# Delta rule and two expert layers on one core: the first chunks' chain in a given order, ten weights loaded at once, and the min of the first block on ScalarE

## The chip, the cores and the metric

One core of one Trainium2 chip runs the kernel. The metric is the device time of one execution in microseconds. The engines are TensorE (PE, with its weight loads as PEld), VectorE (DVE), ScalarE (ACT), GpSimd (POOL) and SyncE (SP), which issues every DMA.

## What is computed

A delta rule over 768 tokens for 4 batches of 8 heads (head size 48), then two expert layers on the 3072 tokens of width 384 that it gives, each through a hidden width of 2048. All in float32.

```python
for t in range(S):
    y[:, :, t] = einsum('bhd,bhde->bhe', q[:, :, t], state)
    v_old = einsum('bhde,bhd->bhe', state, k_n[:, :, t])
    state = state + beta * einsum('bhd,bhe->bhde', k_n[:, :, t], v[:, :, t] - v_old)
# layer 1: g = h where h >= 1, 0 where h <= -1, else (h + 1)**2 / 4
# layer 2: g = max(h, 0)**2;  both: h = x @ w_in, then g @ w_out
```

## The kernel before

The sequence is cut into 24 chunks of 32 tokens; a chunk holds 4 batches x 32 tokens on 128 partitions. Inside a chunk the recurrence is a triangular system. Chunks are taken in groups (`GROUPS`, the first of 2 chunks, the second of 4), and one triangle of 32 x 32 per partition is solved for a whole group by `tri` (L334): a transpose in (`begin`, L351), norms, two scalings (`row`, `row2`), 30 steps of a multiply and an add (`step`, L411 and L412), a transpose out (`end`, L415). Triangle 0 (group 0) is solved by VectorE in two halves of 16 with one instruction for both (`two`), 14 steps of 28 instructions, and the halves are joined by small matmuls (`joined`, L424: `ld` and `dld`, L437 to L450). The other triangles run on GpSimd.

`gram` (L268) makes the k and q products of a chunk on TensorE, and a mask cuts them (L297). For the grams of group 1 and the q halves of chunks 0 and 1, ScalarE first copies the product out (L294) and GpSimd masks the copy. `chunk_steps` (L457) is the chain of a chunk: `ks`, `tr`, `qs`, `pu`, `ku`, `xt`; each is 64 small matmuls and a copy or subtraction by ScalarE or VectorE. Chunks 0 and 1 form block 0 and are done before the first layer starts; chunk 1 takes its dependence on chunk 0 from `cross_gram`.

Layer 1 runs over blocks of 2 or 3 chunks (`SIZES`), for each over 16 slices f of the hidden width: `hidden` (L565) makes one slice with 9 matmuls (a float32 number is held as two parts, so three products) and the activation, and `out1` two slices later multiplies it into the output. Before the change the activation is: ScalarE `r = relu(h + 1)` (L581), VectorE `g = min(r, 2) / 2` (L582), ScalarE `g * g` (L583), VectorE `max(r - 1, g)` (L584), then a ScalarE cast and a VectorE subtraction (L592, L593) for the two parts. The blocks share a ring of three tiles for r and g.

The weights lie in HBM as 64-bit floats. Each of the 32 tiles of layer 1 (16 slices, i = 0 for w_in and 1 for w_out) is loaded by `load_w` and converted in four stages that `flow` staggers by one step each: ScalarE Prelu (L164), two VectorE operations (L172, L175), ScalarE cast (L186), VectorE subtraction (L190). `more_w1` runs one such step. `first1(EAGER)` issues the first 18 loads; each conversion then allows a load up to 8 ahead (`AHEAD`). Layer 1's loads go to the slot of the weight itself; layer 2's to a ring of three raw buffers. The slots of late weights (`spare`) hold the small tiles of the first chunks until then.

The order of the work: up to the norms of triangle 1 every engine issues in the order in which the program is written (`manual_schedule`). After that only TensorE does, and the order on the other engines and on SP is made by a planner from its own model of time. In that part the chain of chunks 0 and 1 runs with 4 x 3 conversion steps between its pieces, then the blocks. Work beside the blocks hangs on slots, two to a slice, 32 to a block: one conversion step a slot in block 0, grams of group 2 at slots 4, 7, 10 and 13, the chains of block 1 from slot 19 (`HEAD`). `later` puts work behind the marked operations `marks[0]` (ScalarE's relu) and `marks[1]` (VectorE's min) on their engines; `tc.issue_after(x)` orders behind x on x's engine and waits for nothing.

Of the kernel before, what the change touches and what calls it, by code (L numbers as in the profile page):

```python
# [25 lines left out]
def kernel(  # L26
# [38 lines left out]
    EAGER = 18  # L65
    AHEAD = 8
# [48 lines left out]
    kqt, kvt, gp, nt, xh, xl = {}, {}, {}, {}, {}, {}  # L115

# [31 lines left out]
    raws = {}  # L148


    def load_w(x, key):
# [30 lines left out]
    def part_stages(key, box):  # L182
# [13 lines left out]
    def weight_items(w):  # L196
# [5 lines left out]
        def item(x):  # L202
            _, f, i = keys[x]
            box = {}
            if w == 0:
                r = part_stages(keys[x], box)
# [4 lines left out]
            r[1] = lambda: (s1(), ahead(x + 1 + (RAW if w else AHEAD)))  # L211
# [5 lines left out]
        def ahead(end):  # L217
            while todo and todo[0][0] < end:
                load_w(*todo.pop(0))
# [48 lines left out]
    def gram(c, lo=0, hi=2, late=0, eng=None):  # L268
# [18 lines left out]
        if c >= KQ:  # L287
            kqg.pop(c)
            if late < 2:
                load_kg(c + KG)  # L290
# [22 lines left out]
    spare = {  # L313
        name: f"w{i}{NF - f}" for name, i, f in
        (("u0", 1, 1), ("u1", 1, 2), ("cross", 0, 1), ("z", 1, 3), ("l", 0, 2), ("d", 1, 4))
    }
# [17 lines left out]
    def tri(n, eng, halves=False):  # L334
# [9 lines left out]
        def two(t, rows, cols):  # L344

            a = t[:, rows, cols]
            (ps_, p_), (rs_, r_), (cs_, c_) = a.ap
            return bass.AP(a.tensor, a.offset, [[ps_, p_], [T2 * (T + 1), 2], [rs_, r_], [cs_, c_]])

# [5 lines left out]
        both = slice(0, T2)  # L355
# [16 lines left out]

        def row():
            if halves:
                d = two(gm, both, both)
                eng.tensor_mul(
                    d, d, r.rearrange("p (a o i) -> p a o i", a=2, o=1)
                    .to_broadcast([P, 2, T2, T2]))
                return
            for e, rs, cs in whole:  # L380
                e.tensor_mul(gm[:, rs, cs], gm[:, rs, cs], across(r, rs, cs))

        def row2():
            if halves:
                eng.tensor_mul(
                    two(x, both, both), two(gm, both, both),
                    g.rearrange("p (a i o) -> p a i o", a=2, o=1).to_broadcast([P, 2, T2, T2]))
            else:
                for e, rs, cs in whole:
                    e.tensor_mul(x[:, rs, cs], gm[:, rs, cs], down(g, rs, cs))  # L390
# [5 lines left out]
        def step(j):  # L396
            if halves:
                w = T2 - 1 - j
                t = ring.tile([P, 2, j, w], F32, tag="t0", bufs=1, name="t")
                rest = two(x, slice(0, j), slice(j + 1, T2))  # L400
                by = two(x, slice(0, j), slice(j, j + 1))
                of = two(gm, slice(j, j + 1), slice(j + 1, T2))
                shape = [P, 2, j, w]
            else:
                w = T - 1 - j
                t = ring.tile([P, j, w], F32, tag="t0", bufs=1, name="t")
                rest = x[:, 0:j, j + 1:T]
                by = x[:, 0:j, j:j + 1]
                of = gm[:, j:j + 1, j + 1:T]
                shape = [P, j, w]  # L410
            eng.tensor_mul(t, by.to_broadcast(shape), of.to_broadcast(shape))  # L411
            eng.tensor_add(rest, rest, t)  # L412
# [150 lines left out]
    marks = [None, None, None]  # L563

    def hidden(layer, n, f):  # L565
# [12 lines left out]
        if layer == 0:  # L578
# [85 lines left out]

    V, G = nc.vector, nc.gpsimd
# [14 lines left out]
    with tc.manual_schedule():  # L680
# [27 lines left out]
        begin, pre, steps, end = tri(0, V, True)  # L708
# [10 lines left out]
        go(masks)  # L719
        end()  # L720
        rows0()
        begin, pre, steps, end1 = tri(1, G)
        begin()
        ins = go(pre[:-2])
        behind[0] = lambda: tc.issue_after(ins.ins)
    ENGINES = {mybir.EngineType.PE}
    with tc.manual_schedule(engines=ENGINES):
        for f in (ld0, dld0):
            for c in range(HEADS):
                f(c)  # L730
        go(pre[-2:])
        go(steps)
        chains = [chunk_steps(c) for c in range(HEADS)]
        (k0, t0, q0, p0, _, x0), (k1, t1_, q1, p1, _, x1) = chains
        for m, fs in enumerate([[k0, t0], [k1], [q0, p0], [t1_], [q1], [x0], [p1], [x1]]):
            go(fs)
            if m < 4:
                more_w1(3)
# [51 lines left out]
        for c in range(HEADS):  # L790
            put(0, 8 + 4 * c, lambda c=c: load_kq(c + KQ))
# [115 lines left out]
```

## Time and profile before

| | |
|---|---|
| median of 3 runs | 1054.86 us (1054.44 to 1056.35) |
| the profiled execution | 1054.6 us |
| its span, first to last instruction | 1052.9 us |
| mean granted TensorE clock | 0.99 of full speed |
| busy in the span | PE 989.3, DVE 611.5, ACT 454.3, POOL 313.2 us |
| all weight loads | 64 of 384 KB, median 6.3 us to land |

A row of the trace has the start in us, the length, the engine, the line, the operation, output<-input and the count; brackets hold the idle time of the engine before it and what ended it, where "issue" means that nothing in the profile was waited for. A row of a group has, after the bar, busy us, mean ns of one, and the idle time before.

### The profile page before, as it was taken

Reading aid. Unit: us, or ns where it says so; the run is one execution under the profiler, and the core shown is the slowest. Engines: PE = TensorE matmul, PEld = TensorE weight load, DVE = VectorE, ACT = ScalarE, POOL = GpSimd, SP = SyncE. Lnnn points to the kernel's source line nnn. Section 1 sums busy time; section 2 is a strip of 40 time slices with the busy share of each in tenths; the row PEclk is TensorE's granted clock in tenths of the full one; section 3 lists DMA queues with packets and bytes.
Section 4 is the critical chain, followed back from the end, with each engine's and each line's share of the span. In section 5 each row is a group of like instructions: output and inputs, shape, how many; then the busy total and the mean of one; then the engine's idle time right before and its main releaser. Section 6 shows DMA issues by size and latency. Waiting matters only on the chain.

```text
span 1052.9 us, 33012 instructions
## 1 busy us (share of the span) xinstructions
PE 989.3 (94%) x14440; PEld 945.0 (90%) x14440; DVE 611.5 (58%) x1125; ACT 454.3 (43%) x931; POOL 313.2 (30%) x456
## 2 busy tenths in 40 slices
PE   4358898999999999999999999999999999999998
PEld 4347788898899998999999999999999999999998
DVE  6879765675575666767545577543434343444333
ACT  2346544445444444545445554433333333333332
POOL 4690681294039208608600123110101010010000
PEclk9997999999999999999999999999999999999999
DMA  9942144352451441512111223010101010000000
GB/s 297 326 121 77 33 124 134 88 150 73 130 152 48 148 134 33 167 56 70 31 42 55 77 90 121 16 45 1 45 1 46 1 45 1 24 1 24 1 23 23
DMA packets 36049, 80.89 MB, mean 77 GB/s; under 512 B 4544, under 2 KB 18368, under 8 KB 35904
## 3 DMA queue, kind: packets, MB, share of 16 engines
q1 hardware_dynamic: 35904, 78.78, 24.8%
q8 instruction: 113, 1.85, 0.8%
q14 instruction: 32, 0.26, 0.1%
HBM read 63.03 MB, written 15.73 MB: 75 GB/s over the span
## 4 chain that ended last, share of the span: by engine, by line
PE 81%; DVE 11%; issue 4%; ACT 2%; DMA 1%; SPq 0%; DVEq 0%; ACTq 0%
PE acc L555 36%; PE h L555 35%; PE tr L486 2%; PE yy L506 2%; PE sps L517 2%; PE yy L472 2%; DVE g L582 1%; DVE g L584 1%; PE g L281 1%; PE ks L472 1%; DVE gl L593 1%; DVE wl L172 1%; DVE wl L175 1%; DVE gp L415 1%; PE xt L540 1%
## 5 line engine op out<-in xcount | busy, mean ns | idle before, releaser
L555 PE MATMUL h<-xh,w 128*128 128x384 f32 (+1 forms) x1632 | 320.4, 332 | 1.8 <-ACT r L581 1.3
L555 PEld LDWEIGHTS h<-xh,w 128*128 128x128 f32 x1632 | 272.7, 190 | 6.8 <-ACT r L581 1.8
L593 DVE TENSOR_TENSOR gl<-g,gh 128x384 fp32r<-128x384 f32 (+1 forms) x272 | 169.5, 623 | 134.3 <-ACT gh L592 128.8
L592 ACT CAST gh<-g 128x384 fp32r<-128x384 f32 (+1 forms) x272 | 135.0, 496 | 209.3 <-DVE g L584 106.0
L555 PE MATMUL h<-xl,w 128*128 128x384 f32 (+1 forms) x816 | 179.8, 329 | 1.3 <-DVE xl L543 1.3
L555 PE MATMUL acc<-gh,w 128*128 128x384 f32 (+1 forms) x864 | 168.5, 331 | 3.8 <-ACT gh L592 3.8
L587 DVE TENSOR_TENSOR g<-r 128x384 f32<-128x384 f32 x128 | 71.4, 558 | 157.4 <-ACT r L586 157.4
L555 PE MATMUL acc<-w,gh 128*128 128x384 f32 x768 | 155.6, 337 | 2.0 <-DVE e L600 2.0
L586 ACT ACTIVATE r<-h,zero 128x384 f32<-128x384 f32 x128 | 74.5, 582 | 166.1 <-PE h L555 166.1
L555 PEld LDWEIGHTS acc<-gh,w 128*128 128x128 f32 x864 | 136.9, 191 | 9.8 <-ACT gh L592 4.2
L555 PEld LDWEIGHTS h<-xl,w 128*128 128x128 f32 x816 | 141.5, 190 | 1.9 <-DVE xl L543 1.9
L555 PEld LDWEIGHTS acc<-w,gh 128*128 128x128 f32 x768 | 136.3, 188 | 2.3 <-ACT gh L592 2.3
L581 ACT ACTIVATE r<-h,one 128x384 f32<-128x384 f32 (+1 forms) x144 | 78.6, 546 | 89.4 <-PE h L555 84.9
L411 POOL TENSOR_TENSOR t<-tx,gm 128x30 f32<-128x30 f32 (+9 forms) x180 | 109.6, 609 | 19.9 <-DVE tx L390 6.4
L412 POOL TENSOR_TENSOR tx<-tx,t 128x30 f32<-128x30 f32 (+9 forms) x180 | 108.4, 602 | 13.7
L584 DVE SCALAR_TENSOR_TENSOR g<-r,g 128x384 f32<-128x384 f32 (+1 forms) x144 | 88.8, 617 | 36.6 <-ACT g L583 34.8
L582 DVE TENSOR_SCALAR g<-r 128x384 f32<-128x384 f32 (+1 forms) x144 | 63.6, 442 | 79.5 <-ACT r L581 78.9
L642 POOL CAST xh<-x2r 128x1152 fp32r<-128x1152 f32 x8 | 9.5, 1186 | 292.9 <-PE h L555 246.1
L583 ACT ACTIVATE g<-g 128x384 f32<-128x384 f32 (+1 forms) x144 | 70.6, 490 | 59.4 <-DVE g L582 58.3
L555 PE MATMUL acc<-gl,w 128*128 128x384 f32 (+1 forms) x432 | 91.5, 320 | 2.6 <-DVE gl L593 2.6
L555 PE MATMUL acc<-w,gl 128*128 128x384 f32 x384 | 88.0, 337 | 0.0
L555 PEld LDWEIGHTS acc<-gl,w 128*128 128x128 f32 x432 | 72.4, 190 | 3.3 <-DVE gl L593 3.3
(94 smaller groups left out, 835.9 us busy)
## 6 DMA issues: line engine op xcount, KB each, us to landing
raw<-in_w_dram SPq DMA_DIRECT2D x64, 384.0 KB, 6.3
kqt<-in_kq_dram SPq DMA_DIRECT2D x88, 192.0 KB, 3.8
kv<-in_kv_dram SPq DMA_DIRECT2D x24, 384.0 KB, 3.1
w2f<-wl SPq DMA_DIRECT2D x32, 192.0 KB, 3.5
w2r<-w2f SPq DMA_DIRECT2D x16, 384.0 KB, 3.0
x2r<-x SPq DMA_DIRECT2D x8, 576.0 KB, 4.4
out_dram<-e SPq DMA_DIRECT2D x24, 192.0 KB, 2.0
x<-e SPq DMA_DIRECT2D x18, 192.0 KB, 2.3
```

The source lines that it names most:

```text
L411: eng.tensor_mul(t, by.to_broadcast(shape), of.to_broadcast(shape))
L412: eng.tensor_add(rest, rest, t)
L472: per_bh(lambda b, h, p, pd: nc.tensor.matmul(o[p, h], kqt[c][pd, b // 2, h, x * T:(x + 1) * T], st[pd, b // 2, h], start=h == 0, stop=x = ...
L555: nc.tensor.matmul(o, *((r, l) if swap else (l, r)), **flags)
L581: marks[0] = nc.scalar.activation(r, h, AF.Relu, bias=one)
L582: marks[1] = nc.vector.tensor_scalar(g, r, 2.0, 0.5, ALU.min, ALU.mult)
L583: nc.scalar.activation(g, g, AF.Square)
L584: nc.vector.scalar_tensor_tensor(g, r, -1.0, g, ALU.add, ALU.max)
L586: marks[0] = nc.scalar.activation(r, h, AF.Relu, bias=zero)
L587: marks[1] = nc.vector.tensor_mul(g, r, r)
L592: nc.scalar.copy(ghi, g)
L593: nc.vector.tensor_sub(glo, g, ghi.bitcast(F32))
```

## The change

In the prelude every engine now keeps the written order through the whole chain of chunks 0 and 1. Ten weights are loaded at first; no other until the eleventh, whose slot (`w14`) is the one that the cross tile uses, and the loads of k, q and v that come later are issued behind that one on SP. From the eighteenth weight (`OWN`) loads go to the ring of three raw buffers. Six conversion steps in place of twelve stand among the chain, and the conversions may run three loads ahead. From the twentieth (`ALONE`) on, the last subtraction of a conversion is GpSimd's. The masks of the prelude are VectorE's. Triangle 0 is solved half by VectorE and half by GpSimd. In block 0 the min becomes `relu(1 - r / 2)` on ScalarE, and the square is taken of one minus that; the mark for `later` is then the VectorE max.

```diff
-    EAGER = 18
-    AHEAD = 8
+    EAGER = 10
+    OWN = 17
+    ALONE = 20
...
-        if w == 0:
+        if w == 0 and x < OWN:
             pool, tag, bufs = wp, f"w{i}{f}", 1
         raw = raws[key] = pool.tile([P, DM, 2], I32, tag=tag, bufs=bufs, name="raw")
-        nc.sync.dma_start(raw.rearrange("p a b -> p (a b)"), (w1, w2)[w][f, i].bitcast(I32))
+        with after[0]():
+            ins = nc.sync.dma_start(
+                raw.rearrange("p a b -> p (a b)"), (w1, w2)[w][f, i].bitcast(I32)
+            )
+        if w == 0 and x == EAGER:
+            after[0] = lambda: tc.issue_after(ins.ins)
...
-            nc.vector.tensor_sub(lo, box["t"], hi.bitcast(F32))
+            (nc.vector if x < ALONE else nc.gpsimd).tensor_sub(lo, box["t"], hi.bitcast(F32))
...
-            r[1] = lambda: (s1(), ahead(x + 1 + (RAW if w else AHEAD)))
+            r[1] = lambda: (s1(), ahead(x + 1 + RAW))
...
         def ahead(end):
+            if w == 0 and turn[0] is not None:
+                end = min(end, EAGER)
...
+    spare = {"cross": f"w1{EAGER // 2 - 1}"}
+    for x, name in enumerate(("u0", "u1", "z", "l", "d", "t")):
+        spare[name] = f"w{x % 2}{NF - 1 - x // 2}"
...
+        parts = whole
+        if halves:
+            parts = [(e, *[slice(T2 * i, T2 * i + T2)] * 2) for i, e in enumerate(halves)]
...
+            for i, e in enumerate(halves or (eng,)):
+                lo, hi = (T2 * i, T2 * i + T2) if halves else (0, T)
+                w = hi - lo - 1 - j
...
+            for e, lo, hi, t in ts:
+                rest = x[:, lo:lo + j, lo + j + 1:hi]
+                e.tensor_add(rest, rest, t)
...
-            marks[1] = nc.vector.tensor_scalar(g, r, 2.0, 0.5, ALU.min, ALU.mult)
-            nc.scalar.activation(g, g, AF.Square)
-            nc.vector.scalar_tensor_tensor(g, r, -1.0, g, ALU.add, ALU.max)
+            if n:
+                marks[1] = nc.vector.tensor_scalar(g, r, 2.0, 0.5, ALU.min, ALU.mult)
+                nc.scalar.activation(g, g, AF.Square)
+            else:
+
+                nc.scalar.activation(g, r, AF.Relu, scale=-0.5, bias=one)
+                nc.scalar.activation(g, g, AF.Square, scale=-1.0, bias=one)
+            last = nc.vector.scalar_tensor_tensor(g, r, -1.0, g, ALU.add, ALU.max)
+            if not n:
+                marks[1] = last
...
-        begin, pre, steps, end = tri(0, V, True)
+        begin, pre, steps, end = tri(0, V, (V, G))
...
-        go([gram(c, late=2, eng=G) for c in range(GFIRST[1], GFIRST[2])])
+        masks1 = [gram(c, late=2) for c in range(GFIRST[1], GFIRST[2])]
         cross_gram(0, 1)
-        masks = [gram(c, 1, 2, late=2, eng=G) for c in range(HEADS)]
+        masks = [gram(c, 1, 2, late=2) for c in range(HEADS)]
         go(steps)
         for c in range(HEADS):
             value(c)
-        go(masks)
+
+        rows0()
         end()
-        rows0()
+        for c in range(HEADS):
+            ld0(c)
+        go(masks1)
+        for c in range(HEADS):
+            dld0(c)
+        chains = [chunk_steps(c) for c in range(HEADS)]
+        (k0, t0, q0, p0, _, x0), (k1, t1_, q1, p1, _, x1) = chains
+        go([k0, t0])
         begin, pre, steps, end1 = tri(1, G)
         begin()
-        ins = go(pre[:-2])
-        behind[0] = lambda: tc.issue_after(ins.ins)
+        go(masks)
+        k1()
+        go(pre[:-2])
+        go([q0, p0, t1_])
+        go(pre[-2:])
+        go(steps)
+        more_w1(2)
+        q1()
+        x0()
+        more_w1(2)
+        p1()
+        more_w1(1)
+        x1()
+        more_w1(1)
...
         turn[0] = None
-        load_kv(HEADS)
+        first1(EAGER + RAW)
+        quiet(load_kv, HEADS)
         for c in range(KG):
-            load_kg(KQ + KG + c)
+            quiet(load_kg, KQ + KG + c)
...
-            put(0, 8 + 4 * c, lambda c=c: load_kq(c + KQ))
+            put(0, 8 + 4 * c, lambda c=c: quiet(load_kq, c + KQ))
```

## Rows read from the trace of the kernel before

**Rows 1.** Stretches: length; busy (count) PE, PEld, DVE, ACT, POOL; clock; DMA share; GB/s.

```profile
27.00:65.70 38.70, 16.24 (x744) 14.13 (x744) 30.23 (x50) 14.60 (x33) 28.74 (x44) 1.00 0.88 266
65.70:81.00 15.30, 9.16 (x161) 8.45 (x161) 15.30 (x25) 6.94 (x16) 13.68 (x23) 0.86 0.26 80
81.00:101.40 20.40, 17.11 (x267) 15.36 (x267) 20.25 (x52) 15.57 (x38) 0.83 (x1) 0.77 0.28 80
101.40:120.00 18.60, 15.39 (x339) 14.33 (x337) 17.54 (x41) 9.40 (x24) 7.53 (x6) 0.91 0.10 24
120.00:138.00 18.00, 17.66 (x538) 16.10 (x538) 8.87 (x20) 8.80 (x21) 15.88 (x28) 1.00 0.26 69
...
58.00:60.00 2.00, 0.91 (x47) 0.72 (x36) 1.67 (x2) 1.21 (x3) 1.84 (x3) 1.00 0.27 106
```

**Rows 2.** TensorE in order of time, 30 to 66 us: start, length, idle before and reason.

```profile
33.07 1.52 PE L437 MATMUL z<-d,l 32*32 32x16 f32 x98 [2.31 <-issue]
41.19 1.52 PE L445 MATMUL w<-gp,z 32*32 32x16 f32 x98 [6.21 <-issue]
48.36 1.00 PE L486 MATMUL tr<-kv,gp 32*32 32x48 f32 x34 [5.03 <-issue]
56.13 0.92 PE L506 MATMUL yy<-u,gp 32*32 32x48 f32 x34 [4.07 <-issue]
60.34 1.00 PE L466 MATMUL yy<-u,cross 32*32 32x48 f32 x35 [1.43 <-issue]
65.68 0.58 PE L555 MATMUL h<-xh,w 128*128 128x256 f32 x1 [0.57 <-ACT xh L542]
```

**Rows 3.** DMA of the first 60 us: the instruction queue; the weight loads (us to landing).

```profile
q8 instruction: 8, 0.13, 1.0%
raw<-in_w_dram SPq DMA_DIRECT2D x32, 384.0 KB, 8.2
```

**Rows 4.** VectorE and GpSimd in order of time, 15 to 27 us.

```profile
15.19 0.18 DVE L411 TENSOR_TENSOR t<-tx,gm 128x28 f32<-128x28 f32 x1
19.64 2.52 POOL L297 TENSOR_TENSOR gp<-gp,mask 128x512 f32<-128x512 f32 x2 [6.41 <-ACT gp L294]
19.67 1.36 DVE L411 TENSOR_TENSOR t<-tx,gm 128x108 f32<-128x108 f32 x1
26.71 0.21 DVE L412 TENSOR_TENSOR tx<-tx,t 128x28 f32<-128x28 f32 x1
```

**Rows 5.** GpSimd by line (busy, mean ns, idle before): 119 to 124, 37.3 to 41.2 us.

```profile
L411 POOL TENSOR_TENSOR t<-tx,gm 128x58 f32<-128x58 f32 x1 | 0.3, 290 | 0.1
L411 POOL TENSOR_TENSOR t<-tx,gm 128x58 f32<-128x58 f32 x1 | 0.5, 480 | 0.1
```

**Rows 6.** VectorE by line: 27 to 65.7 us; after the dots 80 to 101 us.

```profile
L175 DVE SCALAR_TENSOR_TENSOR wl<-wt,wl 128x384 int32<-128x384 int32 x11 | 8.6, 800 | 0.0
L190 DVE TENSOR_TENSOR w<-wl,w 128x384 fp32r<-128x384 f32 x9 | 7.7, 852 | 0.0
L172 DVE TENSOR_SCALAR wl<-raw 128x384 int32<-128x384 uint32 x11 | 6.6, 617 | 0.0
...
L175 DVE SCALAR_TENSOR_TENSOR wl<-wt,wl 128x384 int32<-128x384 int32 x13 | 7.3, 565 | 0.0
L190 DVE TENSOR_TENSOR w<-wl,w 128x384 fp32r<-128x384 f32 x12 | 6.8, 569 | 0.0
L172 DVE TENSOR_SCALAR wl<-raw 128x384 int32<-128x384 uint32 x11 | 3.9, 354 | 0.0
L584 DVE SCALAR_TENSOR_TENSOR g<-r,g 128x256 f32<-128x256 f32 x5 | 2.1, 421 | 0.0
L582 DVE TENSOR_SCALAR g<-r 128x256 f32<-128x256 f32 x5 | 1.5, 296 | 0.0
```

**Rows 7.** ScalarE by line, 65.7 to 101.4 us.

```profile
L581 ACT ACTIVATE r<-h,one 128x256 f32<-128x256 f32 x7 | 3.3, 466 | 2.8 <-PE h L555 2.4 <-DVE gl L593 0.4
```

**Rows 8.** The raw weight tile, 130 to 400 us: its loads.

```profile
DMA to landing us min/median/max: 3.0/3.5/5.3
```

More of the change, by code (lines that the diff above doesn't have):

```diff
@@ L115 @@
     kqt, kvt, gp, nt, xh, xl = {}, {}, {}, {}, {}, {}
+    marks = [None] * 3
     def load_kq(c):
@@ L148 @@
     raws = {}
+    after = [nullcontext]
     def load_w(x, key):
@@ L179, in convert_stages, with part_stages @@
         return [s0, s1]
-    def part_stages(key, box):
+    def part_stages(x, key, box):
         _, f, i = key
@@ L205, in item @@
             if w == 0:
-                r = part_stages(keys[x], box)
+                r = part_stages(x, keys[x], box)
             else:
@@ L288, in gram @@
             kqg.pop(c)
-            if late < 2:
+            if turn[0] is None:
                 load_kg(c + KG)
@@ L311 @@
     cross = {}
[L313 to L316, printed above, removed]
+    spare = {"cross": f"w1{EAGER // 2 - 1}"}
+    for x, name in enumerate(("u0", "u1", "z", "l", "d", "t")):
+        spare[name] = f"w{x % 2}{NF - 1 - x // 2}"
     def cross_gram(a, c):
@@ L332, with tri @@
     T2 = T // 2
-    def tri(n, eng, halves=False):
+    def tri(n, eng, halves=()):
         x = tx
@@ L342, in flat @@
             return t.rearrange("p j i -> p (j i)")[:, diag]
[L344 to L348, printed above, removed]
         def begin():
@@ L371, in gamma2 @@
             return nc.vector.tensor_mul(g, g, bet[:, n, :])
+        parts = whole
+        if halves:
+            parts = [(e, *[slice(T2 * i, T2 * i + T2)] * 2) for i, e in enumerate(halves)]
         def row():
[L374 to L380, printed above, removed]
+            for e, rs, cs in parts:
                 e.tensor_mul(gm[:, rs, cs], gm[:, rs, cs], across(r, rs, cs))
         def row2():
[L384 to L390, printed above, removed]
+            for e, rs, cs in parts:
+                e.tensor_mul(x[:, rs, cs], gm[:, rs, cs], down(g, rs, cs))
             nc.vector.tensor_copy(flat(x), g)
@@ L396, in step @@
         def step(j):
[L397 to L412, printed above, removed]
+            ts = []
+            for i, e in enumerate(halves or (eng,)):
+                lo, hi = (T2 * i, T2 * i + T2) if halves else (0, T)
+                w = hi - lo - 1 - j
+                pool, tag = (wp, spare["t"]) if i else (ring, "t0")
+                t = pool.tile([P, j, w], F32, tag=tag, bufs=1, name="t")
+                ts.append((e, lo, hi, t))
+                e.tensor_mul(
+                    t,
+                    x[:, lo:lo + j, lo + j:lo + j + 1].to_broadcast([P, j, w]),
+                    gm[:, lo + j:lo + j + 1, lo + j + 1:hi].to_broadcast([P, j, w]),
+                )
+            for e, lo, hi, t in ts:
+                rest = x[:, lo:lo + j, lo + j + 1:hi]
+                e.tensor_add(rest, rest, t)
         def end():
@@ L663, in go, with quiet @@
         return r
+    def quiet(load, c):
+        with after[0]():
+            load(c)
     V, G = nc.vector, nc.gpsimd
@@ L718 @@
             value(c)
-        go(masks)
+        rows0()
         end()
-        rows0()
+        for c in range(HEADS):
[6 more added lines that the diff above has]
+        go([k0, t0])
         begin, pre, steps, end1 = tri(1, G)
         begin()
-        ins = go(pre[:-2])
-        behind[0] = lambda: tc.issue_after(ins.ins)
+        go(masks)
[12 more added lines that the diff above has]
+        more_w1(1)
     ENGINES = {mybir.EngineType.PE}
     with tc.manual_schedule(engines=ENGINES):
[L728 to L738, printed above, removed]
         behind[0] = lambda ins=marks[2]: tc.issue_after(ins.ins)
         turn[0] = None
-        load_kv(HEADS)
+        first1(EAGER + RAW)
+        quiet(load_kv, HEADS)
         for c in range(KG):
-            load_kg(KQ + KG + c)
+            quiet(load_kg, KQ + KG + c)
         SL = 2 * NF
```

2 lines of the change are left out of this document (removed).

## The prediction

> **What bounds the kernel now.** I read the table of busy time by stretch first [rows 1]. From 120 us on TensorE is busy 17.66 of 18.00 us, so there is nothing to win behind that point except what is carried into it: whatever is saved before it shifts the rest. Up to 65.7 us, where the first block's first matmul starts [rows 2], it is another kernel: TensorE is busy 16.24 of 38.70 us, the DMA engines have a share of 0.88, and VectorE, busy 30.23, is the fullest engine. From 65.7 to 101.4 VectorE has no gap worth the name (15.30 of 15.30, 20.25 of 20.40), and TensorE's granted clock falls to 0.86 and 0.77 of 2.4 GHz. So there are two limits: first a chain with waits in it, then VectorE's backlog of weight conversions.
>
> The second view is TensorE's own order of time [rows 2]. Five times between 30 and 60.4 us it stops with "issue" as the reason: 2.31, 6.21, 5.03, 4.07 and 1.43 us, 19.1 in all. They recur after 128 matmuls (98 and 30 of a stage), and the queue marked "instruction" moved 8 packets in the first 60 us [rows 3]. I read these stops as TensorE waiting for its next piece of program, while the weight loads, 8.2 us from issue to landing there [rows 3], fill the same DMA engines. The share is 0.88 over the stretch; around the last and shortest stop the loads have thinned to 0.27 [rows 1].
>
> **The change, part by part.**
>
> Triangle of group 0. Its steps run on VectorE from 15.19 to 26.92 us [rows 4]: 11.7 us for 28 instructions. That is not their own length: one of 1.36 us lies exactly beside a mask on GpSimd [rows 4]. Now VectorE does one half and GpSimd the other, and the masks are gone from GpSimd. GpSimd is the slower: a 58-element step is 0.29 us plus 0.10 of gap with VectorE at ease, 0.48 plus 0.10 with VectorE at conversions [rows 5]. So 28 instructions take between 10.9 and 16.2 us; VectorE's own load is small here, so I take 0.42 each, 11.8. **No gain: the steps still end near 27** (ends 26 and 31.4).
>
> From there to the first hidden matmul: 38.7 us before (26.9 to 65.7). With ten weights instead of eighteen to twenty-six the loads end in the middle twenties, and the eleventh load sits on the slot of the cross tile, so no load runs until the chain has used that tile. I take out the 19.1 us of stops and leave one at 1.43, the shortest. The six masks move to VectorE and stand in front of the chain's subtractions: four of 512 columns at an estimated 0.7 (a 256-column operation is 0.42 [rows 6]) and two at 0.4 add 3.6. The conversions that stood between the chain's steps are now behind the chain or beside it. 38.7 - 19.1 + 1.4 + 3.6 = 24.6, so the **first block starts at 51.6 instead of 65.7**. Ends: 47.5 if the masks hide under the matmuls, 69.3 if every stop stays.
>
> Moved past on the queues: the loads of v for chunk 2 and of k and q for chunks 6 to 9 now go out behind the eleventh weight, so not before the chain's last use of the cross tile. The first of them is wanted two tiles into block 0, some 10 us later, and a load lands in 3.5 us [rows 8]: nothing. What is queued behind a marked operation in block 0 now follows the chain's last VectorE operation but one instead of the min, which keeps the 2 us transposes out of the chain: left at nothing, on the side of a gain.
>
> First half of block 0. VectorE had converted 11 weights by 65.7 [rows 6]; now 5 are begun by then. Until hidden tile 7 it has some 15 weights and 7 activation chains to do. A weight costs 0.62 + 0.80 + 0.85 = 2.27 us while GpSimd is at its triangle and 0.35 + 0.57 + 0.57 = 1.49 without it [rows 6], less about 0.08 each by which neighbours overlap: 1.24. The removed min costs 0.30 [rows 6], so a chain is left with two operations, 0.68 net at ease; I take 1.0 beside GpSimd. GpSimd was busy 28.74 and then 13.68 us [rows 1], some 40 of it with triangle 1, and nearly idle after 81; starting near 42 it lasts to about 82. From 51.6 to 82: 30.4 us less two masks of 0.7 is 29.0, at 2 x 2.27 + 1.0 = 5.5 a tile 5.3 tiles and 10.6 weights. The rest: 4.4 x 1.24 + 1.7 x 0.68 + 1.4 for two masks = 8.0. VectorE is through at **90 instead of 101.4: 11.4 us are left** of the 14.1.
>
> Second half. Twelve weights instead of about three remain; their subtractions go to GpSimd, which was busy 0.83 of 20.40 and 7.53 of 18.60 us [rows 1]. Even at twice VectorE's 0.57, 12 x 1.14 = 13.7 us fit, if in part beside triangle 2; I cost them at nothing, and without that cover they would delay single weights by a microsecond each. VectorE gains about as much as it loses: 12 x 0.75 in place of 3 x 1.24, less 9 x 0.30. ScalarE pays: 9 weights more, two passes of 384 columns each, and 9 tiles with one activation of 256 for the min. The nearest row is the Relu that is there, 0.47 [rows 7]; I take it for all 27, 12.7, less overlap some 11 us on top of 18.2 of 36.6 [rows 1]. It has the room, but it serves the activation chain in order. Between nothing and 11 I take a third, **3.8 given back**, since ScalarE stays at four fifths.
>
> The row for the min says 0.30 on VectorE against 0.47 on ScalarE. The Trainium skill (ScalarE: Activation LUTs, Rules for kernel authors) says that relu, max and min belong on VectorE; by it the 16 moved operations cost 16 x 0.17 = 2.7 us where ScalarE is the limit, and the sum would be that much worse. The stretches show VectorE full and ScalarE not, so I don't follow it.
>
> Sum: -14.1 at the start, +2.7 of it lost in the first half (14.1 to 11.4), +3.8 in the second: -7.6. The profiled execution took 1054.6 us (its span is 1052.9), 0.3 under the median shown, 1054.86. **Forecast 1047.0 us.**
>
> **Rivals.**
>
> Nothing is given back. ScalarE and the loads keep up, and the first block starts at 50: 1054.6 - 13 = about 1041. For it: TensorE ran freely wherever VectorE had slack (17.66 of 18.00). Against: 101.4 to 120 shows VectorE at 17.54 of 18.60 already.
>
> VectorE's work is merely moved. Between 27 and 101.4 it idles less than 9 us, so an earlier start without less work returns everything: 1054, no change. It holds if the split triangle or the ordered chain leaves VectorE idle by as much as it saves, 9 to 11 us.
>
> Weights arrive late (slower). From the eighteenth on, weights load into three raw buffers. A load goes out when the weight three before it is converted: landing, a ScalarE pass of about 0.5, VectorE's 0.92. With 3.5 us to land, the median of the later loads [rows 8], three weights cycle in 5.0 us; the second half's pace (9 tiles in 36.6 us) asks for three in 6.1. It decides at 4.6 us of landing and queueing; 5.3 occurs [rows 8], and SP's queue is in order, with k and q loads in it that wait for TensorE. At the 8.2 of the crowded stretch [rows 3] the cycle is 9.7: 15 weights take 48.5 instead of 30.5, and -11.4 + 18 = +6.6: 1061. ScalarE would then wait in its conversion with the activations behind it.
>
> The stops stay. The last stop of the five came where the loads had thinned, so a fetch has a price of its own; if it is 4 us each, the first block starts at 69.3, meets 12.7 us of GpSimd's triangle, and VectorE is through at 101 after all: +3.8, 1058.4. The Trainium skill (DMA: Bandwidth & Descriptors, Queues, rings and completion order) says that an engine serves its queues in turn, packet by packet; by that a fetch is not held up by the length of the weight queue, and fewer weights would not shorten it. The stops of 5 and 6 us in the full stretch against 1.43 at a share of 0.27 speak against it.
>
> **How the numbers follow.** Forecast case (1043 to 1052): 0.45. Nothing given back: 0.17. Merely moved: 0.13. Late weights: 0.16. Stops stay: 0.09. About 0.2% (2.1 us) is what a measurement of this kernel can tell from no change. Faster: the first two, 0.62. No change: 0.13. Slower: the last two, 0.25. The range runs from 1039 (start at 47.5, nothing returned) to 1060, and leaves out the far ends of the two outer cases, everything won and weights late throughout.
>
> **What would show it.** Right: the first hidden matmul near 51 us with at most two stops under 2 us before it; no weight loads between about 25 us and the chain's end; the new Relu on ScalarE near 0.47 and no min on VectorE in block 0; VectorE's first idle time in block 0 near 90. Wrong: triangle 0 ending past 31; stops of 4 us with idle DMA engines; ScalarE waiting for a raw weight in block 0; a first hidden matmul earlier than before but block 1 no earlier.

## The result, and the profile after

The changed kernel takes **1064.6 us** (median of 4 runs, 1063.69 to 1068.93) against 1054.93 for the kernel before on the same chip (4 runs): ratio 1.0098, 95% interval 1.0068 to 1.0127. It is slower; the forecast was 1047.0 with a range that ended at 1060. The profiled execution has a span of 1062.5 us, 9.6 more than the 1052.9 of before, at a mean granted clock of 0.975.

The gain at the start is there, and it is lost twice afterwards. TensorE in order of time, in the kernel after (start, length, idle before and its reason, as [rows 2]; `h` is a tile of the hidden layer):

```profile
27.76 1.54 PE L292 MATMUL g<-kqt 48*32 48x32 f32 x97 [2.95 <-issue]
29.22 0.61 PE L433 MATMUL z<-d,l 32*32 32x16 f32 x30
31.36 1.51 PE L433 MATMUL z<-d,l 32*32 32x16 f32 x98 [1.53 <-issue]
34.97 1.51 PE L441 MATMUL w<-gp,z 32*32 32x16 f32 x97 [1.69 <-issue]
38.85 1.00 PE L482 MATMUL tr<-kv,gp 32*32 32x48 f32 x35 [1.74 <-issue]
46.49 0.61 PE L462 MATMUL yy<-u,cross 32*32 32x48 f32 x36 [1.59 <-issue]
52.86 0.58 PE L551 MATMUL h<-xh,w 128*128 128x256 f32 x1 [0.84 <-ACT xh L538]
...
72.98 1.01 PE L551 MATMUL acc<-gl,w 128*128 128x256 f32 x3 [5.30 <-DVE gl L595]
...
109.36 0.97 PE L551 MATMUL h<-xh,w 128*128 128x256 f32 x6
...
146.31 1.09 PE L551 MATMUL h<-xh,w 128*128 128x256 f32 x5 [3.66 <-POOL w L199]
...
150.29 0.87 PE L551 MATMUL h<-xh,w 128*128 128x256 f32 x6
```

And three rows of the same view of the kernel before:

```profile
30.14 0.61 PE L437 MATMUL z<-d,l 32*32 32x16 f32 x30 [1.66 <-DVE d L433]
...
110.11 0.97 PE L555 MATMUL h<-xh,w 128*128 128x256 f32 x6
...
137.93 0.84 PE L555 MATMUL h<-xh,w 128*128 128x256 f32 x6
```

From 30 us on, the stops of 19.1 us are now 6.6, and the first hidden matmul starts at 52.86 instead of 65.68: 12.8 us won. Tile 10 of block 0, the eleventh of its 16 slices, starts at 109.36 against 110.11: nearly all of it is gone. Block 1 starts at 150.29 against 137.93: 12.4 us behind. From there to the end 2.8 come back. So there are two losses of 12 and 13 us, one before tile 10 and one after it.

Busy time by stretch, kernel after (columns as in [rows 1]):

```profile
27.00:52.90 25.90, 14.92 (x744) 13.16 (x744) 14.14 (x31) 7.84 (x19) 7.64 (x14) 0.90 0.20 62
52.90:81.00 28.10, 17.09 (x272) 15.65 (x276) 28.10 (x39) 14.72 (x33) 24.35 (x34) 0.61 0.81 200
81.00:99.40 18.40, 13.94 (x237) 12.20 (x227) 18.40 (x35) 12.15 (x28) 12.15 (x20) 0.72 0.46 139
99.40:120.00 20.60, 15.80 (x271) 14.07 (x270) 16.38 (x33) 12.97 (x30) 10.06 (x12) 0.83 0.34 109
120.00:150.30 30.30, 21.27 (x540) 19.29 (x539) 17.71 (x27) 16.78 (x39) 28.50 (x41) 0.89 0.43 122
```

From 52.9 to 99.4 VectorE has no gap at all (28.10 of 28.10, 18.40 of 18.40), while it idled 11.8 of the 25.9 us ahead of that. GpSimd, in the same view, is the engine beside it. Its triangles, kernel after (last instruction of triangle 0; first and last of triangle 1), and then the first and last instruction of triangle 1 in the kernel before:

```profile
23.65 0.22 POOL L408 TENSOR_TENSOR tx<-tx,t 128x14 f32<-128x14 f32 x1
...
46.58 0.23 POOL L401 TENSOR_TENSOR t<-tx,gm 128x30 f32<-128x30 f32 x1
...
92.71 0.47 POOL L408 TENSOR_TENSOR tx<-tx,t 128x30 f32<-128x30 f32 x1
```

```profile
37.41 0.48 POOL L411 TENSOR_TENSOR t<-tx,gm 128x30 f32<-128x30 f32 x1 [1.43 <-DVE tx L390]
...
80.29 0.66 POOL L412 TENSOR_TENSOR tx<-tx,t 128x30 f32<-128x30 f32 x1
```

Triangle 1 ran from 37.4 to 81.0 before, 28 us of that beside the chain with its stops and 15.3 beside block 0. Now 40.3 us of it lie beside block 0. VectorE by line in those 40.3 us (52.9 to 93.2; after the bar busy us, mean ns), against [rows 6]:

```profile
L184 DVE SCALAR_TENSOR_TENSOR wl<-wt,wl 128x384 int32<-128x384 int32 x16 | 13.4, 845 | 0.1
L199 DVE TENSOR_TENSOR w<-wl,w 128x384 fp32r<-128x384 f32 x15 | 13.1, 875 | 0.0
L181 DVE TENSOR_SCALAR wl<-raw 128x384 int32<-128x384 uint32 x16 | 11.1, 705 | 0.0
L584 DVE SCALAR_TENSOR_TENSOR g<-r,g 128x256 f32<-128x256 f32 x4 | 2.6, 653 | 0.0
...
L308 DVE TENSOR_TENSOR gp<-g,mask 128x512 f32<-128x512 f32 x2 | 1.4, 678 | 0.0
```

What ended the waits from 99 to 152 us, kernel after (us in total, times, longest):

```profile
ACT w L195 <- DVE wl L184: 7.7, 6, 2.5
...
ACT wt L173 <- DMA raw<-in_w_dram: 5.8, 4, 2.3
...
PE xt L536 <- ACT kv L506: 4.0, 1, 4.0
...
PE h L551 <- POOL w L199: 3.7, 1, 3.7
```

### The profile page after: what moved, and what is told of

Same layout as the page of the kernel before. It is cut to its first block, busy times and chain, and to the rows that moved or that the text cites. A ratio compares the mean times of both kernels' runs of the same rounds, so it can differ in the third digit from the quotient of the medians.

```text
span 1062.5 us, 33036 instructions
## 1 busy us (share of the span) xinstructions
PE 995.8 (94%) x14440; PEld 949.6 (89%) x14440; DVE 611.4 (58%) x1103; ACT 460.8 (43%) x947; POOL 328.0 (31%) x492
## 4 chain that ended last, share of the span: by engine, by line
PE 82%; DVE 8%; issue 4%; POOL 3%; DMA 2%; ACT 1%; SPq 0%; DVEq 0%; ACTq 0%; POOLq 0%
PE acc L551 36%; PE h L551 35%; PE g L292 2%; PE tr L482 2%; PE yy L502 2%; PE yy L468 2%; PE sps L513 1%; PE ks L468 1%; DVE wl L181 1%; DVE gl L595 1%; DMA kqt<-in_kq_dram 1%; POOL t L401 1%; POOL tx L408 1%; DVE g L584 1%; DVE wl L184 1%
## 5 line engine op out<-in xcount | busy, mean ns | idle before, releaser
L595 DVE TENSOR_TENSOR gl<-g,gh 128x384 fp32r<-128x384 f32 (+1 forms) x272 | 172.3, 633 | 132.0 <-ACT gh L594 130.7
L594 ACT CAST gh<-g 128x384 fp32r<-128x384 f32 (+1 forms) x272 | 134.4, 494 | 209.1 <-DVE g L584 105.0
L551 PEld LDWEIGHTS acc<-gh,w 128*128 128x128 f32 x864 | 137.9, 193 | 10.5 <-ACT gh L594 4.6
L408 POOL TENSOR_TENSOR tx<-tx,t 128x84 f32<-128x84 f32 (+18 forms) x194 | 112.7, 581 | 14.5
L401 POOL TENSOR_TENSOR t<-tx,gm 128x84 f32<-128x84 f32 (+18 forms) x194 | 110.6, 570 | 18.1 <-DVE tx L387 4.0
L584 DVE SCALAR_TENSOR_TENSOR g<-r,g 128x384 f32<-128x384 f32 (+1 forms) x144 | 90.8, 630 | 39.7 <-ACT g L579 33.7
L578 DVE TENSOR_SCALAR g<-r 128x384 f32<-128x384 f32 (+1 forms) x128 | 55.8, 436 | 73.4 <-ACT r L576 72.5
L579 ACT ACTIVATE g<-g 128x384 f32<-128x384 f32 (+1 forms) x128 | 63.8, 498 | 54.4 <-DVE g L578 53.5
```

Of the source, the lines that this page charges most:

```text
L401: e.tensor_mul(t, x[:, lo:lo + j, lo + j:lo + j + 1].to_broadcast([P, j, w]), gm[:, lo + j:lo + j + 1, lo + j + 1:hi].to_broadcast([P, j, w]),
L408: e.tensor_add(rest, rest, t)
L551: nc.tensor.matmul(o, *((r, l) if swap else (l, r)), **flags)
L584: last = nc.vector.scalar_tensor_tensor(g, r, -1.0, g, ALU.add, ALU.max)
L594: nc.scalar.copy(ghi, g)
L595: nc.vector.tensor_sub(glo, g, ghi.bitcast(F32))
```

## The experiments

The theories. **The triangle's place**: its steps beside VectorE's backlog slow it, and the chain's waits had been their cover. **The weights left over**: VectorE idles in the shortened chain, so more conversions fall into the second half and hold ScalarE's order up. Its rivals for the second half are **late loads** and **GpSimd's subtractions**. **ScalarE's min** lengthens the activation. And the stops: do they come from the weight loads?

All results, each against the kernel before on the same chip (1055.1, 1054.34, 1054.2 and 1053.57 us in the four groups of runs):

| kernel | us | ratio, 95% interval |
|---|---|---|
| changed | 1064.60 | 1.0098, 1.0068 to 1.0127 |
| changed, loads eight ahead | 1061.10 | 1.0052, 1.0032 to 1.0073 |
| changed, subtractions on VectorE | 1064.21 | 1.0100, 1.0063 to 1.0137 |
| changed, min on VectorE | 1067.08 | 1.0120, 1.0096 to 1.0144 |
| changed, eighteen loads at once | 1066.70 | 1.0118, 1.0093 to 1.0142 |
| changed, without triangle 1's steps | 1048.90 | 0.9948, 0.9928 to 0.9967 |
| before, without triangle 1's steps | 1049.08 | 0.9952, 0.9937 to 0.9967 |
| changed, triangle 1 earlier | 1059.73 | 1.0051, 1.0035 to 1.0066 |
| the same, loads eight ahead | 1056.69 | 1.0024, 1.0005 to 1.0044 |
| that, last six subtractions on VectorE | 1055.61 | 1.0016, 1.0001 to 1.0030 |
| earlier, loads ahead, ten weight steps | 1054.25 | 1.0000, 0.9989 to 1.0010 |
| that, last six subtractions on VectorE | 1052.89 | 0.9994, 0.9980 to 1.0007 |
| the same with eight weight steps | 1056.80 | 1.0029, 1.0017 to 1.0041 |
| changed, ten weight steps alone | 1061.55 | 1.0080, 1.0065 to 1.0096 |
| before, triangle 1 later | 1072.00 | 1.0184, 1.0165 to 1.0203 |

**Loads eight ahead.**

```diff
-    OWN = 17
+    OWN = 32
-            r[1] = lambda: (s1(), ahead(x + 1 + RAW))
+            r[1] = lambda: (s1(), ahead(x + 1 + (RAW if w else 8)))
```

> The changed kernel with all 32 weights of the first layer's own tiles kept in their own raw slots and eight loads ahead instead of three; nothing else is touched. Two theories. (A) Late weights: in the second half of block 0 ScalarE waited some 6.6 us for raw weights, and each wait pushes the activations behind it; then these waits go, block 1 starts 5 to 8 us earlier than at 150.3, and the time falls from 1064.6 to 1057 to 1060. (B) The backlog rules: the weights come late only because VectorE and ScalarE reach them late, or the earlier loads bring the instruction stops back; then the time stays within 2 us of 1064.6, and the waits for raw weights are gone while VectorE or GpSimd ends the wait in their place.

1061.1, 3.5 us less by the medians, between the two forecasts. ScalarE's waits for raw weights are gone from that stretch, but block 1 still starts only at 146.2 (4.1 us earlier), and TensorE's wait for GpSimd's subtraction grows:

```profile
PE h L551 <- POOL w L199: 4.8, 1, 4.8
```

Late loads are a part, the smaller one; as (B) said, GpSimd ends a wait in their place.

**Subtractions on VectorE.**

```diff
-    ALONE = 20
+    ALONE = 32
```

> The changed kernel with all subtractions of weights on VectorE again, none on GpSimd. (A) GpSimd's subtractions, 1.0 us each and queued between the steps of triangle 2, are what the last hidden tiles of block 0 wait for (one wait of 3.66 us): then block 1 starts 3 to 5 us earlier and the time is 1060 to 1062. (B) VectorE was relieved by them, 12 at 0.55 us and beside GpSimd's triangle more: then the end of block 0 moves later by up to 6 us and the time is 1066 to 1070. (C) Neither, the loads set the pace: 1063 to 1066.

1064.2: no difference, as (C) said. TensorE's wait for GpSimd is gone, and at 131.4 it waits 7.31 us for ScalarE's copy `kv` instead of 3.99. What stands last is replaced at once.

**Min on VectorE.**

```diff
-            if n:
+            if True:
...
-            if not n:
-                marks[1] = last
```

> The changed kernel with min(r, 2) / 2 on VectorE in block 0 as before, everything else as changed. (A) VectorE's backlog is the bound of the first half, so 16 more operations of 0.3 to 0.5 us there cost 4 to 6 us: 1068 to 1071. (B) ScalarE is the bound of the second half and its order holds the chain (two passes after each other on the same engine, each waiting for the previous one's result): then the time falls by 2 to 4 us, to 1060 to 1063. If both hold in their halves, 1063 to 1066.

1067.1: above the 1063 to 1066 of "both hold", below the 1068 of (A), and not where (B) alone has it; the interval overlaps that of the changed kernel. ScalarE's min is not what costs the 10 us.

**Eighteen loads at once.**

```diff
-    EAGER = 10
-    OWN = 17
+    EAGER = 18
+    OWN = 19
```

> The changed kernel with eighteen weights loaded at once in place of ten, as before. (A) TensorE's instruction stops before the first hidden matmul are long where weight loads fill the DMA engines: the stops of 1.5 to 1.7 us grow back to 3 to 6 us, the first hidden matmul moves from 52.9 to 58 or later; as VectorE's backlog behind it is the bound in the first half, at most half of it shows in the time. (B) The stops depend on the number of matmuls since the last fetch alone: the first hidden matmul stays within 1 us of 52.9, and the time is that of the changed kernel, or up to 3 us less because eight more weights are there early.

The first hidden matmul starts at 55.6, 2.8 us later, by one stop that grew while loads filled the DMA engines. TensorE in order, and the stretch 27 to 40 us of this kernel:

```profile
33.56 1.51 PE L433 MATMUL z<-d,l 32*32 32x16 f32 x98 [3.99 <-issue]
```

```profile
27.00:40.00 13.00, 6.13 (x382) 5.67 (x383) 3.21 (x6) 1.28 (x4) 0.00 (x0) 1.00 0.52 198
```

The same stretch of the changed kernel, with its stops of 1.53 to 1.74:

```profile
27.00:40.00 13.00, 7.13 (x417) 6.48 (x417) 4.65 (x8) 1.39 (x5) 0.00 (x0) 1.00 0.03 6
```

The stop that grew is the only one that fell into the loads (in the 4.06 us ahead of 33.56 the DMA share is 0.92); the later ones, with the DMA engines idle, are 1.69, 1.74 and 1.82. So (A) holds for a stop beside loads, and the first matmul comes between the two forecasts. The difference in time is not resolved.

**Both kernels without triangle 1's steps.**

```diff
-        go(steps)
+        go(steps[:1])
```

> The changed kernel with all steps of triangle 1 but the first left out (part of the computation is missing: group 1's triangular inverse isn't formed, and nothing else is). It is read against its twin, the kernel before with the same left out. (A) The lost first half is GpSimd's triangle running beside VectorE's backlog: without it VectorE's weight operations fall from 0.65 to 0.82 us to 0.35 to 0.57, its first idle time comes near 87 instead of 99, and the time falls to 1053 to 1057, while the twin gains far less, 2 to 5 us from 1054.9, since two thirds of its triangle lay beside the waiting chain: the two come out within 4 us of each other. (B) The triangle is not it: both gain alike, and the changed kernel stays 8 to 10 us behind its twin.

> The kernel before with the same steps of triangle 1 left out. (A) Only the last 15 of its 43 us lay beside VectorE's backlog: the time falls by 2 to 5 us, to 1050 to 1053. (B) As much as in the changed kernel, 8 to 11 us, to 1044 to 1047, if a triangle costs the same wherever it lies.

1048.90 and 1049.08: the changed kernel gains 15.7 us by the medians, the kernel before 5.3, and the two are level. The 10 us between the kernels hang on the triangle. VectorE by line from 52.9 to 99.4 us in the changed kernel without it:

```profile
L184 DVE SCALAR_TENSOR_TENSOR wl<-wt,wl 128x384 int32<-128x384 int32 x19 | 10.4, 553 | 0.0
L199 DVE TENSOR_TENSOR w<-wl,w 128x384 fp32r<-128x384 f32 x18 | 10.0, 554 | 0.0
L181 DVE TENSOR_SCALAR wl<-raw 128x384 int32<-128x384 uint32 x21 | 7.2, 355 | 3.0 <-DMA raw<-in_w_dram 3.0
...
L584 DVE SCALAR_TENSOR_TENSOR g<-r,g 128x256 f32<-128x256 f32 x10 | 4.2, 423 | 0.0
L308 DVE TENSOR_TENSOR gp<-g,mask 128x512 f32<-128x512 f32 x4 | 2.7, 686 | 0.0
```

845, 875 and 705 ns became 553, 554 and 355. The gain is larger than (A) had it, by 4 us in the changed kernel and 1 in its twin. And a second thing: without the triangle, a first block that starts 13.6 us earlier (52.9 against 66.5) brings nothing at all. Tile 10 and block 1, in the changed kernel without the triangle and then in the kernel before without it:

```profile
94.31 0.98 PE L551 MATMUL h<-xh,w 128*128 128x256 f32 x6
...
134.65 0.87 PE L551 MATMUL h<-xh,w 128*128 128x256 f32 x6
```

```profile
104.98 0.97 PE L555 MATMUL h<-xh,w 128*128 128x256 f32 x6
...
134.12 0.84 PE L555 MATMUL h<-xh,w 128*128 128x256 f32 x6
```

At tile 10 the changed kernel is still 10.7 us ahead, at block 1 it is 0.5 behind. So triangle 1 makes most of the first loss (without it tile 10 moves from 109.4 to 94.3, in the kernel before from 110.1 to 105.0), and the second, 11.2 us here, is there without it. My reading of the second: the chain's waits had been time in which VectorE converted weights; removed, the conversions are done later. The runs with ten weight steps try it.

**Triangle 1 earlier.**

```diff
-        for c in range(HEADS):
-            ld0(c)
         go(masks1)
+        begin, pre, steps, end1 = tri(1, G)
+        begin()
+        go(pre[:1])
+        for c in range(HEADS):
+            ld0(c)
+        go(pre[1:])
+        go(steps)
         for c in range(HEADS):
             dld0(c)
```

(and the same lines removed from behind `k0`, `t0` and `k1`).

> The changed kernel with triangle 1 written right after the first six masks' first four, ahead of the subtractions of the chain, so that GpSimd begins its steps near 35 us instead of 46.6, beside VectorE's waits for the chain; nothing is left out. (A) What counts is how much of the triangle lies beside the backlog: its steps end near 78 instead of 93, VectorE's first idle time comes 3 to 5 us earlier, and the time falls to 1059 to 1062. (B) The chain itself pays: the triangle's transposition and scalings (some 3 us of VectorE) and the shared engine time stand ahead of the chain's subtractions, the first hidden matmul moves from 52.9 to 56 or later, and the time stays at 1063 to 1066.

1059.7, as (A) said, with the first hidden matmul at 53.6. GpSimd, this kernel, first and last instruction of triangle 1:

```profile
35.76 0.23 POOL L401 TENSOR_TENSOR t<-tx,gm 128x30 f32<-128x30 f32 x1
...
76.33 0.46 POOL L408 TENSOR_TENSOR tx<-tx,t 128x30 f32<-128x30 f32 x1
```

**Triangle 1 later, in the kernel before.**

```diff
-        go(pre[-2:])
-        go(steps)
         chains = [chunk_steps(c) for c in range(HEADS)]
...
         behind[0] = lambda ins=marks[2]: tc.issue_after(ins.ins)
+        with behind[0]():
+            go(pre[-2:])
+            go(steps)
```

> The kernel before with the last scaling and all steps of triangle 1 issued only behind the chain's last subtraction, so that GpSimd begins them near 67 us instead of 37.4; nothing is left out or added. (A) The triangle's place is the price: then VectorE's operations from 66 us on are slow as in the changed kernel (0.65 to 0.82 us a weight operation instead of 0.47 to 0.63), the chain ahead of it becomes 0 to 4 us shorter, and the kernel before loses 6 to 12 us in all: 1061 to 1066, as the changed kernel does. (B) The place doesn't matter, since the time of the chain beside a triangle is as dear as that of the backlog: 1052 to 1057.

1072.0: beyond what (A) gave, and far from (B). GpSimd, and VectorE by line from 70.7 to 116 us, in this kernel:

```profile
70.67 0.28 POOL L411 TENSOR_TENSOR t<-tx,gm 128x30 f32<-128x30 f32 x1 [1.64 <-DVE tx L390]
...
115.46 0.47 POOL L412 TENSOR_TENSOR tx<-tx,t 128x30 f32<-128x30 f32 x1
```

```profile
L175 DVE SCALAR_TENSOR_TENSOR wl<-wt,wl 128x384 int32<-128x384 int32 x18 | 15.0, 833 | 0.0
L190 DVE TENSOR_TENSOR w<-wl,w 128x384 fp32r<-128x384 f32 x16 | 12.8, 797 | 0.0
L172 DVE TENSOR_SCALAR wl<-raw 128x384 int32<-128x384 uint32 x16 | 9.8, 615 | 0.0
```

Nothing but the place of the triangle differs from the kernel before. The loss lies ahead of tile 10, which starts 18.2 us later; block 1 is 18.1 behind. The price can now be put together from the four places; the loss is the difference of the ratio to that of the kernel without the steps, times 1054.9 us (for "changed, earlier" too, the changed kernel without the steps stands in):

| kernel | triangle 1 beside block 0 | loss by it | per us |
|---|---|---|---|
| before | 65.7 to 81.0: 15.3 us | 5.1 us | 0.33 |
| changed, earlier | 53.6 to 76.8: 23.2 us | 10.9 us | 0.47 |
| changed | 52.9 to 93.2: 40.3 us | 15.8 us | 0.39 |
| before, later | 70.7 to 115.9: 45.3 us | 24.5 us | 0.54 |

Each microsecond of triangle beside the backlog costs a third to a half of one; four points don't show one fixed price. Beside the chain with its stops it cost nothing: in the kernel before, VectorE's three weight operations take 800, 852 and 617 ns from 27 to 65.7 us [rows 6] and 560, 554 and 442 without the triangle, and yet the first hidden matmul starts at 65.7 with it and at 66.5 without.

**Earlier, and loads eight ahead.** Both diffs together.

> The two edits that could help together: triangle 1 earlier, and eight loads ahead with a raw slot for each of the 32 weights (the loads alone gave 1061.1 against 1064.6). If the two add, as two separate halves of block 0 would: 1056 to 1059. If the earlier triangle only moves the wait to GpSimd's subtractions: 1060 to 1062.

1056.7: the two add, within what the intervals tell.

**And the last six subtractions on VectorE.**

```diff
-            (nc.vector if x < ALONE else nc.gpsimd)
+            (nc.gpsimd if ALONE <= x < 26 else nc.vector)
```

> Triangle 1 earlier and eight loads ahead (together 1056.7), and the subtractions of weights 26 to 31 back on VectorE, those of 20 to 25 left on GpSimd. In the kernel without this edit TensorE waited 5.41 us at 136.5 for a subtraction that GpSimd did between the steps of triangle 2, while VectorE was busy 11.5 of 25 us there. (A) That wait holds the end of block 0: 1052 to 1054. (B) The hops of late weights between VectorE and ScalarE hold it, and the subtraction only came last among several: 1055.5 to 1057.

1055.6, as (B) said, and not told from the kernel without the edit.

**Ten weight steps in the chain**, on top of earlier and loads ahead.

```diff
         go(masks)
+        more_w1(2)
         k1()
-        go([q0, p0, t1_])
+        q0()
+        more_w1(1)
+        go([p0, t1_])
         more_w1(2)
...
         p1()
-        more_w1(1)
+        more_w1(2)
```

> Triangle 1 earlier and eight loads ahead (together 1056.7), and four more of the weight steps put between the chain's steps, so that ten instead of six are written ahead of block 0: VectorE idled some 10 us in that stretch, while four weights cost it 6 to 10 us later beside GpSimd's triangle. (A) The changed kernel starts block 0 early with a backlog of unconverted weights, and that backlog is what gives the gain back: the chain becomes 0 to 3 us longer, tile 3 starts some 4 us earlier than at 73.2, the second half has four fewer weights to wait for, and the time falls to 1048 to 1053, under both kernels. (B) The backlog is not the bound, or the chain grows by as much as the weights cost: 1055 to 1059.

1054.25, between (A) and (B), level with the kernel before. The mechanism shows in the stretch from tile 10 to block 1. This kernel, then the changed one, then the one before:

```profile
109.30:138.90 29.60, 24.40 (x695) 22.19 (x692) 17.94 (x32) 17.85 (x41) 24.63 (x36) 0.94 0.16 43
```

```profile
109.40:150.30 40.90, 28.81 (x695) 26.20 (x692) 26.43 (x41) 21.93 (x50) 35.61 (x50) 0.83 0.42 120
```

```profile
110.10:137.90 27.80, 24.25 (x698) 22.16 (x691) 18.14 (x40) 12.80 (x31) 22.10 (x33) 0.94 0.17 46
```

With earlier triangle and loads alone the stretch took 38.9 us, with the ten steps 29.6:

```profile
102.00:140.90 38.90, 26.68 (x694) 24.27 (x691) 24.12 (x41) 21.60 (x51) 33.89 (x47) 0.88 0.13 39
```

But the first hidden matmul moved from 52.3 to 58.2 and tile 10 from 102.0 to 109.3: of the 9.3 us that the stretch lost, 7.3 only moved ahead of it, and block 1 starts 2.0 us earlier. The work was put back into the chain, and the chain grew with it.

These lines also show TensorE's clock, which the forecast left out. The changed kernel's 695 matmuls take 28.81 us at a granted clock of 0.83, the 698 of the kernel before 24.25 at 0.94: up to 4.6 of the 13.1 us of the second loss are slower matmuls. Six matmuls of a tile took 0.97 us at 138.0, where the granted clock was 1.00, the upper of its two levels (2.4 and 1.2 GHz), and 1.50 us at 131.9, where it was 0.60, most of the time the lower one; TensorE had waited 3.99 us up to 128.6 and been busy since. No run here separates the clock from the waits that it follows.

**The same, last six subtractions on VectorE**, and **eight weight steps** instead of ten; the second against the first:

```diff
         p1()
-        more_w1(2)
         x1()
```

> Both edits on top of the earlier triangle and the eight loads ahead: ten weight steps ahead of block 0, and the last six subtractions on VectorE. If the two losses are separate, as much as both gave alone, 1046 to 1051. If more weights ahead already take the last ones out from between triangle 2's steps, the same as with the ten weight steps alone, within 1.5 us.

> Earlier triangle, eight loads ahead, last six subtractions on VectorE, and eight weight steps in the chain instead of ten (1052.9 with ten, 1055.6 with six). With ten, the second chunk's copy and cast waited 4.8 and 4.1 us behind weight steps. If these waits cost time, 1050 to 1052; if VectorE's whole work from 40 us on sets the end, it lies between its neighbours, 1053 to 1055.

1052.89 and 1056.80. The first stays within 1.5 us of the kernel without the last edit, the second of the two cases named. It is the fastest of all that compute everything, yet not told from the kernel before (0.9980 to 1.0007), so no version was found that is faster than that one. The second lies outside its neighbours, 1052.9 and 1055.6, and neither reading explains it. Every edit lets the planner order the engines anew, which may be why; no run shows it. Edits worth a few microseconds aren't ranked here.

**Ten weight steps alone**, in the changed kernel.

> The changed kernel with ten weight steps instead of six between the steps of the chain, and nothing else (the triangle stays where it is, the loads three ahead). (A) VectorE's idle 11 us ahead of the first hidden matmul are what the second half pays for: the wait moves to the chain by 2 to 5 us, the stretch from hidden tile 10 to block 1 falls from 41 us to about 30, and the time to 1056 to 1061. (B) Four weights sooner only move the backlog, or meet GpSimd's triangle all the same: 1062 to 1066.

1061.55, between (A) and (B), and its interval overlaps that of the changed kernel. The stretch from tile 10 to block 1 falls to 32.1 us, near the 30 of (A):

```profile
112.50:144.60 32.10, 25.47 (x702) 23.17 (x692) 18.42 (x34) 18.10 (x43) 25.84 (x38) 0.89 0.34 101
```

But tile 10 itself comes at 112.5, 3.1 us later; block 1 starts at 144.6, 5.7 earlier. GpSimd stood still inside the triangle, for a load of v that its queue had ahead of the next step, and the triangle ended at 107.7:

```profile
91.00 0.83 POOL L268 TENSOR_TENSOR kv<-kv,nt 128x384 f32<-128x384 f32 x1 [9.11 <-DMA kv<-in_kv_dram]
```

## Why the prediction was wrong, step by step

| point | before | forecast | measured |
|---|---|---|---|
| triangle 0 ends | 26.9 | 27 | 23.9 |
| first hidden matmul | 65.7 | 51.6 | 52.9 |
| VectorE's first idle time | 101.4 | 90 | 99.4 |
| block 1 starts | 137.9 | 130.3 (137.9 - 7.6) | 150.3 |

In the profiled executions the forecast's sum comes out like this: -12.8 at the start (forecast -14.1), +10.8 up to VectorE's first idle time (+2.7), +14.4 from there to block 1 (+3.8), and -2.8 behind it (nothing): +9.6 instead of -7.6.

**Triangle 0** ended 3 us sooner than "no gain" said, outside the ends of 26 to 31.4. The two engines went in step, 28 instructions each in 9.5 us or 0.34 us for one; I had 0.42. Little of it reached the chain: `z`, the first matmul on the solved triangle, starts at 29.22 against 30.14, because TensorE, in its fixed order, first sat through a stop of 2.95 us and a gram (VectorE had `d` ready at 24.4). In the kernel before, the same stop ended at 26.94, beside the triangle's last steps.

**From there to the first block** the total was right, 12.8 us won of 14.1 forecast, but partly by luck. The stretch behind triangle 0 took 29.0 us and not 24.6. One stop of 1.43 was forecast; from 30 us on there are four, 6.6 us in all, 5.1 too many. Against that stand `z`, 0.9 us earlier, and the masks: with the stops and `z` taken off, 0.6 us of added time is left for them and everything else, where 3.6 were forecast. That weight loads lengthen the stops was read rightly (the rival that the stops stay at 4 us is refuted): with eighteen loads one of them grows to 3.99. What was not foreseen is that 1.5 to 1.7 us of each remain with a DMA share of 0.03.

**The first half of block 0** is the step that failed first: "VectorE is through at 90 instead of 101.4: 11.4 us are left". It was 99.4, so 2.0 were left. The price of a weight beside the triangle, 2.27 us, was nearly right: 845, 875 and 705 ns make 2.43. Two terms of it were mis-sized. The triangle lasted until 93.2 and not 82, from 46.6 instead of "near 42" and for 46.6 us instead of 40 (it took 41.0 us where it began at 35.8). And VectorE did 19 weights by its first idle time, not 15. Behind both stands what the forecast never counted as a cost of the edit: the stops were the triangle's cover. In the kernel before, 28 of its 43.5 us lay ahead of the first block; TensorE stood at its stops for 14 of them, VectorE was busy 20.5, and the conversions that the triangle slowed there held nothing up, as the kernel without it shows.

**The second half** missed by more: "a third, 3.8 given back". From VectorE's first idle time to block 1 it took 50.9 us instead of 36.5: 14.4 given back. From tile 10 on VectorE's line of two-operand conversions ran 9 times instead of 3. The forecast added busy times and found room on each engine. Its sum for VectorE was wrong by itself: 12 x 0.75 is 9.0, and 3 x 1.24 plus 9 x 0.30 are 6.4, so VectorE had 2.6 us more to do and not "about as much". But VectorE was busy only 26.4 of the 40.9 us behind tile 10, so this isn't the main part. Each of these weights goes ScalarE, VectorE, ScalarE, and then GpSimd or VectorE, in queues that also hold the activations and the next chunk's chain; the list of waits fits that, though taking away one of them (loads, subtractions) let the next stand last. With four weight steps moved ahead the stretch falls from 40.9 to 32.1 us in the changed kernel and from 38.9 to 29.6 with the other two edits, at the price of a later tile 10. The late loads, a rival of mine, are some 3.5 us of it; the subtractions on GpSimd, costed at nothing, show no difference in time when taken away alone.

**The min**: back on VectorE it didn't help (1067.1 against 1064.6, not resolved), so the call is not refuted and not shown to be a gain. The new Relu took 505 ns on ScalarE, 0.47 was forecast.

**Of the rivals**, none gave 1064.6 alone. "VectorE's work is merely moved" (1054, chance 0.13) is what the two kernels without the triangle show: 13.6 us earlier, same time. The changed kernel is that, plus the triangle. Its condition was in the text, that the ordered chain leaves VectorE idle by as much as it saves, and the rows fit it: VectorE's work ahead of the first block fell from 30.2 of 38.7 us [rows 1] to 14.1 of 25.9, with 11.8 idle. Two of the forecast's own signs of being wrong came true: ScalarE waits for raw weights in block 0, and the first hidden matmul is earlier but block 1 isn't.

**What stays open**: how the 13 us after tile 10 divide between queues that are held up, VectorE's operations beside triangle 2 (L184 took 966 ns there in the mean) and TensorE's lower clock, and whether a schedule exists that keeps the early start without the triangle beside the backlog.

## What to carry to other kernels

Before removing a wait, list what the other engines did during it, and price that work at its new place: here the removed stops had held both weight conversions and the triangle. If another engine has no gap behind the wait, an earlier start keeps only what that engine's work allows: here 2.0 of the 12.8 us were left at VectorE's first idle time. And where two engines slow each other, count the microseconds that they lie side by side before and after: here the triangle lay 25 us longer beside the backlog, at 0.33 to 0.54 us each an estimated 8 to 13.5, and 10.7 were measured. It is one of two losses; the other came from the work left over.

## What the runs showed of the hardware

The operations of VectorE are not all slowed by GpSimd. Beside the triangle those whose operands all lie in SBUF took 1.5 to 2 times as long (L184 845 against 553 ns, L199 875 against 554, L584 653 against 423), while the mask of a product that is read from PSUM (L308) took 678 against 686. The Trainium skill (SBUF — State Buffer, Who interferes with whom) states that a VectorE instruction with two inputs in SBUF contends with a GpSimd instruction that reads SBUF and one with at most one SBUF input doesn't, outside certain faster modes; the trace agrees for these four. L181, with a single SBUF input, was slowed most (705 against 355), so by the page it would have to be in such a mode; no run here shows which.

An "issue" stop of TensorE in the chain has a part that no DMA traffic explains: 1.53 to 1.74 us in the changed kernel and 0.45 to 1.43 in the one with the earlier triangle and loads ahead, at shares of 0.02 to 0.03. Beside loads it is longer: 3.99 us with eighteen loads at once (share 0.92 in that stretch), up to 6.21 in the kernel before, whose share was 0.88 from 27 to 65.7 us [rows 1, 2].
